# Turning k, q and x on VectorE in 32x32 squares instead of on TensorE

## The chip, the cores and the metric

The kernel runs on one core of one Trainium2 chip. The metric is the device time of one execution in microseconds (us). The clock that TensorE was granted differs a little from execution to execution (0.991 to 1.000 of full speed over the runs of the kernel before), and with it the time, by about 0.5%.

Names: PE is TensorE, ACT ScalarE, DVE VectorE, POOL GpSimd, and SP the engine whose queue issues nearly all DMA transfers. A "chunk" is 128 consecutive time steps of one batch entry; there are 24, counted from 0. The kernel works in steady blocks, one a chunk, from chunk 6 on; what comes before is the start.

## The reference

An mLSTM cell with a stabilised exponential gate, and behind it a feed-forward layer with a squared ReLU.

```python
B, H, S, D = 4, 8, 768, 40
for t in range(S):
    m_new = maximum(f_gate[t] + m, i_gate[t])
    f_stab, i_stab = exp(f_gate[t] + m - m_new), exp(i_gate[t] - m_new)
    C = f_stab * C + i_stab * outer(v[t], k[t])        # per batch entry and head
    n = f_stab * n + i_stab * k[t]
    y[t] = sigmoid(o_gate[t]) * (C @ q[t]) / maximum(abs(n @ q[t]), 1)
x = y.transpose(0, 2, 1, 3).reshape(B * S, H * D)      # 3072 x 320
h = maximum(x @ w_in, 0)                               # w_in 320 x 2048
out = (h * h) @ w_out                                  # w_out 2048 x 320
```

## The kernel before

The recurrence is computed chunk by chunk as attention with decay weights: scores of k and q, a product with the weights, and a state C carried from chunk to chunk. For the scores k and q are needed with the head dimension on the partitions, for the feed-forward layer x with its features there. TensorE makes all three by transposing against an identity matrix.

```python
def load(s):                      # k, q, v of one chunk, each [128 time steps, 8 heads, 40]
    b, c = divmod(s, NB)
    for dst, src in load_parts(s):
        nc.sync.dma_start(dst, src[b, :, c * P : (c + 1) * P, :].rearrange("h p d -> p h d"))

def transposes(s, o=(False, False)):
    d = st[s]
    for i, n in enumerate(("kT", "qT")):
        tp = bank(o[i])
        for j in range(PR):       # PR = 4 pairs of heads
            nc.tensor.transpose(tp[:, j, :], d["kq"][:, i, 2 * j : 2 * j + 2, :]..., ident[:])
        d[n] = work.tile([P, PR, P], F32, name=n)
        (nc.scalar.copy if ... else nc.vector.tensor_copy)(d[n][:], tp)

def turn_rows(s):
    ...
    for a in range(3):
        nc.tensor.transpose(tp[:, a, :], d["x"][:, a * P : (a + 1) * P], ident[:])
    nc.scalar.copy(st["xT", g][:, :, j * P : (j + 1) * P], tp[:])
```

The input weights arrive as raw words in 26 pieces, through a ring of buffers. ACT makes `mag` and `low` of a raw piece, DVE and POOL join them to a rounded fp32 piece, and then the next piece is fetched into the ring:

```python
def fetch(self):                  # next raw piece, on the SP queue
    ... nc.sync.dma_start(to, src)
def words(self):                  # ACT: abs and copy of the raw words -> mag, low
    ...
def join(self):                   # DVE x3, POOL x1 -> rounded piece; then
    ... self.fetch()

def attend_on(s):                 # second quarter of every steady block
    do(attend, s)
    do(normalise, s)
    do(load, s + 4)
    ...
for n, (which, g, i) in enumerate(parts):     # 4 quarters a block
    s, at = 6 + n // 4, n % 4
    ...
    if at == 1: attend_on(s)
    if at == 3:
        do(turn_rows, s)
        do(transposes, s + 1)
    ...                           # a quarter of the feed-forward products
    if n < 4:                     # chunk 6: the last pieces of the weights
        while rounding.done < NEXT[8 + n]:
            rounding.step()
```

So fetches of weights go on into chunk 6's block, on the same SP queue as all loads of chunks. The queue's timelines below show its issues in program order.

## Time and profile before

| | before |
|---|---|
| time, median of 3 | 568.83 us (568.2 to 569.38) |
| span of the profiled execution, granted clock | 565.8 us, 0.999 |
| PE busy | 554.9 us, 98% |
| one odd and one even block together | 44.1 us |
| scores of chunk 8 start at | 144.04 us |

PE is the bound: a product stands behind every other one and nothing waits, from 68 us on.

In the SP queue's timeline (start, duration of the issue, line, transfer) at the end of the start, the last piece of raw weights is issued like this:

```profile
104.77 0.57 SPq L268 DMA_DIRECT2D kq<-in_q_dram  x1
105.44 1.95 SPq L268 DMA_DIRECT2D va<-in_v_dram  x1
114.33 0.34 SPq L174 DMA_DIRECT2D raw<-in_moe_w_out_dram  x1
116.11 0.37 SPq L286 DMA_DIRECT2D A_bc<-a_rows  x1
```

The queue has nothing to do from 107.4 to 114.3 us: it is waiting for a ring buffer to come free (6.9 us behind DVE's last use of one, in the list of the queue's waits).

### The profile page before, as it was taken

The numbers are of one execution on the slowest core, as the hardware profiler recorded it, in microseconds if no ns is written. First come the engines' busy times: TensorE is split into PE (matmuls) and PEld (weight loads), VectorE is DVE, ScalarE is ACT, GpSimd is POOL, SyncE is SP. The second block draws the span as 40 slices with busy tenths as digits, with TensorE's granted clock in tenths as the row PEclk, the third lists the DMA queues.
The fourth block names the chain that finished last, engine by engine and source line by source line (L and its number), as shares of the span: only waits on it lengthen the run. The fifth ranks groups of instructions, "written<-read, shape, count | busy, mean of one in ns | idle before, by whom it ended". The sixth has DMA issues, their size and how long they took to land.

```text
span 565.8 us, 9740 instructions
## 1 busy us (share of the span) xinstructions
PE 554.9 (98%) x3878; PEld 497.8 (88%) x3879; DVE 312.0 (55%) x602; ACT 193.1 (34%) x483; POOL 98.1 (17%) x113
## 2 busy tenths in 40 slices
PE   9988899999999999999999999999999999999997
PEld 5876788887889989989989989989988998989997
DVE  8689978685554454455464364265356355434441
ACT  3767677353162033242131423223315105011000
POOL 3356543142112100111131120101211210000000
PEclk9999999999999999999999999999999999999999
DMA  9997989824313351233231433331411000000000
GB/s 193 222 215 166 171 191 202 169 60 85 57 39 48 79 91 25 64 81 48 61 66 39 89 48 62 73 58 38 76 34 38 1 23 2 1 24 0 25 24 23
DMA packets 130909, 42.60 MB, mean 75 GB/s; under 512 B 101072, under 2 KB 127696, under 8 KB 130864
## 3 DMA queue, kind: packets, MB, share of 16 engines
q1 hardware_dynamic: 130768, 41.79, 36.1%
q8 instruction: 30, 0.49, 0.4%
q10 hardware_dynamic: 96, 0.20, 0.1%
q14 instruction: 15, 0.12, 0.1%
HBM read 37.95 MB, written 4.03 MB: 74 GB/s over the span
## 4 chain that ended last, share of the span: by engine, by line
PE 92%; DVE 4%; ACT 1%; issue 1%; DMA 1%; POOL 0%; POOLq 0%; SPq 0%; DVEq 0%
PE h_ps L555 30%; PE h_ps L461 28%; PE h_ps L472 8%; PE hp L400 7%; PE tp L363 4%; PE tp L350 3%; PE h_ps L501 3%; PE dC L393 3%; PE hi L386 3%; PE tp L445 1%; PE idle L621 1%; PE A_ps L302 1%; ACT W_sb L326 1%; DVE mag L198 1%; PE A_ps L298 1%
## 5 line engine op out<-in xcount | busy, mean ns | idle before, releaser
L461 PE MATMUL h_ps<-xT,w_in 128*128 128x256 f32 x768 | 176.7, 383 | 2.3 <-POOL w_in L203 1.8
L461 PEld LDWEIGHTS h_ps<-xT,w_in 128*128 128x128 f32 x768 | 142.2, 190 | 25.1 <-issue 3.0
L487 ACT ACTIVATE r_sb<-h_ps 128x512 f32<-128x512 f32 x96 | 49.9, 601 | 173.8 <-PE h_ps L472 170.6
L494 DVE TENSOR_TENSOR g<-r_sb 128x512 f32<-128x512 f32 x96 | 62.4, 708 | 69.5 <-ACT r_sb L487 69.5
L555 PE MATMUL h_ps<-w_out,g 128*128 128x160 f32 x528 | 76.9, 302 | 0.0
L555 PEld LDWEIGHTS h_ps<-w_out,g 128*128 128x128 f32 x528 | 72.5, 190 | 1.3 <-ACT r_sb L487 0.3
L326 ACT ACTIVATE W_sb<-A_bc,b_T 128x128 f32<-128x128 f32 x176 | 53.8, 394 | 5.9 <-POOL A_bc L311 5.9
L555 PE MATMUL h_ps<-T,S 128*128 128x160 f32 x352 | 51.4, 299 | 0.0
L472 PE MATMUL h_ps<-xT,w_in 64*128 64x256 f32 x384 | 49.0, 391 | 0.0
L555 PEld LDWEIGHTS h_ps<-T,S 128*128 128x128 f32 x352 | 49.0, 190 | 0.0
L472 PEld LDWEIGHTS h_ps<-xT,w_in 64*128 64x128 f32 x384 | 34.8, 186 | 12.3 <-issue 9.3
L337 POOL TENSOR_TENSOR vw<-va,W_sb 128x328 f32<-128x328 f32 x20 | 16.6, 828 | 165.3 <-ACT W_sb L326 138.5
L400 PE MATMUL hp<-va,P_sb 128*128 128x41 f32 x368 | 44.1, 280 | 0.0
L400 PEld LDWEIGHTS hp<-va,P_sb 128*128 128x128 f32 x368 | 42.9, 192 | 0.0
L569 DVE TENSOR_TENSOR y_sb<-y_sb,h_ps 128x160 f32<-128x160 f32 x33 | 10.6, 320 | 55.1 <-PE h_ps L555 55.1
L419 POOL TENSOR_TENSOR C_sb<-C_sb,Cd 128x328 f32<-128x328 f32 x16 | 14.5, 904 | 140.1 <-DVE C_sb L411 139.9
L375 DVE TENSOR_TENSOR P_sb<-tp,W_sb 128x512 f32<-128x512 f32 x46 | 29.5, 683 | 13.0 <-PE tp L363 12.5
L569 DVE TENSOR_TENSOR y_sb<-h_ps,y_sb 128x160 f32<-128x160 f32 x22 | 7.1, 324 | 49.6 <-PE h_ps L555 30.9
L578 ACT COPY y_sb<-h_ps 128x160 f32<-128x160 f32 x11 | 3.2, 292 | 70.6 <-PE h_ps L555 70.6
L363 PEld LDWEIGHTS tp<-qT,kT 40*128 40x128 f32 x384 | 24.2, 187 | 3.3 <-issue 1.6
L363 PE MATMUL tp<-qT,kT 40*128 40x128 f32 x384 | 26.9, 279 | 0.0
L446 ACT COPY xT<-tp 128x384 f32<-128x384 f32 x24 | 11.4, 477 | 43.2 <-PE tp L445 43.2
(96 smaller groups left out, 682.5 us busy)
## 6 DMA issues: line engine op xcount, KB each, us to landing
A_bc<-a_rows SPq DMA_DIRECT2D x22, 512.0 KB, 4.4
raw<-in_moe_w_out_dram SPq DMA_DIRECT2D x16, 320.0 KB, 3.7
raw<-in_moe_w_in_dram SPq DMA_DIRECT2D x8, 512.0 KB, 5.2
kq<-in_k_dram SPq DMA_DIRECT2D x24, 160.0 KB, 4.4
kq<-in_q_dram SPq DMA_DIRECT2D x24, 160.0 KB, 4.9
va<-in_v_dram SPq DMA_DIRECT2D x24, 160.0 KB, 4.5
og<-in_o_gate_dram SPq DMA_DIRECT2D x24, 160.0 KB, 4.2
out_dram<-y_sb SPq DMA_DIRECT2D x24, 160.0 KB, 1.8
```

The costliest lines, as they stand in the source:

```text
L326: nc.scalar.activation(d["W"][:, i * n + h, :], A[i][:, h, :], AF.Exp, bias=b_T[:, b, c, i * n + h : i * n + h + 1],)
L350: nc.tensor.transpose(tp[:, j, :], d["kq"][:, i, 2 * j : 2 * j + 2, :].rearrange("p h d -> p (h d)"), ident[:],)
L363: nc.tensor.matmul(sc[i][:, j, :], lhsT=d["kT"][rows, j, :], rhs=d["qT"][rows, j, :], start=True, stop=True,)
L375: nc.vector.tensor_tensor(t, d["sc"][i], d["W"][:].rearrange("p (j two) t -> p j two t", two=2)[:, :, i, :], op=ALU.mult,)
L386: nc.tensor.matmul(hi[:, 2 * j : 2 * j + 2, :].rearrange("p h d -> p (h d)"), lhsT=d["qT"][:, j, :], rhs=C[:, j].rearrange("p h d -> p (h ...
L400: nc.tensor.matmul(hp[:, h, :], lhsT=d["P"][h % 2][:, h // 2, :], rhs=d["va"][:, h, :], start=True, stop=True,)
L461: nc.tensor.matmul(hs[i][:, n, :], lhsT=w_in[:, a, fb * P : (fb + 1) * P], rhs=xT[:, a, :], start=(n == 0 and a == 0), stop=False,)
L472: nc.tensor.matmul(hs[i][:, n, :], lhsT=w_in2[rows, 2 * pp + n, :], rhs=xT[rows, 2, :], start=False, stop=(n == 1),)
L487: nc.scalar.activation(rs[-1][:], h[:], AF.Relu)
L494: nc.vector.tensor_tensor(g4[:, :, i, :], r[:], r[:], op=ALU.mult)
L555: nc.tensor.matmul(to, lhsT=lhsT[:, p], rhs=rhs[:, p, :], start=(start and p == 0), stop=(p == NPAIR - 1), skip_group_check=True,)
L569: add = lambda to, a, b: nc.vector.tensor_tensor(to, a, b, op=ALU.add)
```

## The change

The intent is to take the transposes off PE. VectorE's transpose turns each 32x32 square in itself (the prediction names the page), so the loads put each square where it belongs, and one VectorE instruction then turns every square of a tile, those of k and x in place. For k and q, from chunk 7 on, a copy from DRAM to DRAM first sorts the rows by pairs of heads (`pair_up`), four loads for each of the two fetch the squares. For x, from chunk 6 on, the finished rows are stored to DRAM and fetched back as squares by four loads. Core of the diff:

```diff
+    def pair_up(s):
+        b, c = divmod(s, NB)
+        for n, src in enumerate((k, q)):
+            nc.sync.dma_start(
+                kq_d[s, n].rearrange("two j t d -> two j (t d)"),
+                src[b, :, c * P : (c + 1) * P, :].rearrange("(j two) t d -> two j (t d)", two=2),
+            )
+    def squares_in(s, n, dst):
+        for i in range(2):
+            for e in range(0, D, SQ):
+                ... nc.sync.dma_start(dst[...], kq_d[s, n, i, :, :, e : e + w].rearrange("j (m r) a -> r (j m) a", r=SQ))
+    def turn_kq(s):
+        nc.vector.transpose(kT, kT);  nc.vector.transpose(qT, q_squares(s))      # shortened
+    def store_rows(s):
+        nc.sync.dma_start(x_d[s]..., st[s]["x"]...)
+        for r in range(P // SQ):
+            nc.sync.dma_start(t[r * SQ : (r + 1) * SQ]..., x_d[s, :, :, r * SQ : (r + 1) * SQ]...)
+    def turn_squares(s):
+        nc.vector.transpose(t, t)
     def attend_on(s):
         do(attend, s)
         do(normalise, s)
+        do(store_rows, s)
+        do(load_kT, s + 2)
         do(load, s + 4)
+        do(pair_up, s + 5)
 ...  # the start, chunks 3 to 5
             load_A(s + 2)
+            for r in {3: (7, 8), 5: (9,), 7: (10,)}.get(u, ()):
+                pair_up(r)
             for r in {1: (4,), 3: (5, 6), 5: (7,), 7: ()}[u]:
                 load(r)
 ...  # the steady blocks
         if at == 3:
-            do(turn_rows, s)
-            do(transposes, s + 1)
 ...
         if at == 2:
             do(weigh_on, s + 1)
+            do(turn_kq, s + 1)
+        if at == 3:
+            do(turn_squares, s)
```

More of the change, by code (lines that the diff above doesn't have):

```diff
@@ L90 @@
     A_d = nc.dram_tensor("a_rows", (BH, S), F32, kind="Internal").ap()
+    kq_d = nc.dram_tensor("kq_rows", (NT, 2, 2, PR, P, D), F32, kind="Internal").ap()
+    x_d = nc.dram_tensor("x_rows", (NT, 3, P, P), F32, kind="Internal").ap()
     NKQ = 4
@@ L95 @@
     va_b = [consts.tile([P, H, D1], F32, name=f"va{i}") for i in range(NKQ)]
+    NKT = 3
+    kT_b = [consts.tile([P, PR, P], F32, name=f"kT{i}") for i in range(NKT)]
     ident = consts.tile([P, P], F32)
@@ L263, in load_parts, with q_squares, load_kT @@
         return (kq[:, 0, :, :D], k), (kq[:, 1, :, :D], q), (va[:, :, :D], v)
+    SQ = 32
+    KQ_SQ, X_SQ = 7, 6
+    def pair_up(s):
[8 more added lines that the diff above has]
+            for e in range(0, D, SQ):
+                w = min(SQ, D - e)
+                nc.sync.dma_start(
+                    dst[DP * i + e : DP * i + e + SQ].rearrange("p (b a) -> p b a", a=SQ)[:, :, :w],
+                    kq_d[s, n, i, :, :, e : e + w].rearrange("j (m r) a -> r (j m) a", r=SQ),
+                )
+    def q_squares(s):
+        return kq_b[s % NKQ][:, 1].rearrange("p h d -> p (h d)")
     def load(s):
         b, c = divmod(s, NB)
-        for dst, src in load_parts(s):
+        (dk, sk), nat_q, vv = load_parts(s)
+        for dst, src in ((dk, sk), nat_q, vv) if s < KQ_SQ else ((dk, sk), vv):
             nc.sync.dma_start(dst, src[b, :, c * P : (c + 1) * P, :].rearrange("h p d -> p h d"))
+        if s >= KQ_SQ:
+            if s < KQ_SQ + NKQ:
+                nc.gpsimd.memset(q_squares(s), 0.0)
+            squares_in(s, 1, q_squares(s))
+    def load_kT(s):
+        t = st[s]["kT"] = kT_b[s % NKT]
+        squares_in(s, 0, t[:].rearrange("p j t -> p (j t)"))
+    def turn_kq(s):
+        d = st[s]
+        nc.vector.transpose(d["kT"][:].rearrange("p j t -> p (j t)"), d["kT"][:].rearrange("p j t -> p (j t)"))
+        d["qT"] = work.tile([P, PR, P], F32, name="qT")
+        nc.vector.transpose(d["qT"][:].rearrange("p j t -> p (j t)"), q_squares(s))
     def load_o(s):
@@ L352, in transposes @@
                 )
-            d[n] = work.tile([P, PR, P], F32, name=n)
+            d[n] = work.tile([P, PR, P], F32, name=n) if i else kT_b[s % NKT]
             (nc.scalar.copy if i == 0 or s in (0, *range(2, 7)) else nc.vector.tensor_copy)(d[n][:], tp)
@@ L436, in normalise, with xT_half @@
         nc.vector.tensor_copy(x[:, DM:], x[:, DM - KR : DM])
+    def xT_half(s):
+        g, j = divmod(s, GT)
+        if j == 0:
+            st["xT", g] = xts.tile([P, GT, 3, P], F32, name="xT")
+        return st["xT", g][:, j]
+    def store_rows(s):
+        t = st[s]["xT"] = xT_half(s).rearrange("p c t -> p (c t)")
+        nc.sync.dma_start(x_d[s].rearrange("c t d -> t c d"), st[s]["x"][:].rearrange("p (c d) -> p c d", c=3))
+        for r in range(P // SQ):
+            nc.sync.dma_start(
+                t[r * SQ : (r + 1) * SQ].rearrange("p (b a) -> p b a", a=SQ),
+                x_d[s, :, :, r * SQ : (r + 1) * SQ].rearrange("c (n p) a -> p (c n) a", p=SQ),
+            )
+    def turn_squares(s):
+        t = st[s]["xT"]
+        nc.vector.transpose(t, t)
+        del st[s]
     def turn_rows(s):
         d = st[s]
-        g, j = divmod(s, GT)
-        if j == 0:
-            st["xT", g] = xts.tile([P, 3, WG], F32, name="xT")
+        t = xT_half(s)
         tp = ps_at.tile([P, 3, P], F32, name="tp", tag="at")
@@ L445, in turn_rows @@
             nc.tensor.transpose(tp[:, a, :], d["x"][:, a * P : (a + 1) * P], ident[:])
-        nc.scalar.copy(st["xT", g][:, :, j * P : (j + 1) * P], tp[:])
+        nc.scalar.copy(t, tp[:])
         del st[s]
@@ L461, in ffn1_main @@
                     nc.tensor.matmul(
-                        hs[i][:, n, :], lhsT=w_in[:, a, fb * P : (fb + 1) * P], rhs=xT[:, a, :],
+                        hs[i][:, n, :], lhsT=w_in[:, a, fb * P : (fb + 1) * P], rhs=xT[:, :, a, :],
                         start=(n == 0 and a == 0), stop=False,
@@ L472, in ffn1_rest @@
                 nc.tensor.matmul(
-                    hs[i][:, n, :], lhsT=w_in2[rows, 2 * pp + n, :], rhs=xT[rows, 2, :],
+                    hs[i][:, n, :], lhsT=w_in2[rows, 2 * pp + n, :], rhs=xT[rows, :, 2, :],
                     start=False, stop=(n == 1),
@@ L609, in attend_on @@
         do(normalise, s)
+        do(store_rows, s)
+        do(load_kT, s + 2)
         do(load, s + 4)
+        do(pair_up, s + 5)
         if 8 <= s < 20:
             load_o(s + 4)
-    zeros = consts.tile([P, W], BF16)
+    zeros = consts.tile([P, 16], BF16)
     nc.vector.memset(zeros[:], 0.0)
@@ L620, in idle @@
         for _ in range(n):
-            nc.tensor.matmul(t[:], lhsT=zeros[:, :P], rhs=zeros[:], start=True, stop=True)
+            nc.tensor.matmul(
+                t[:], lhsT=zeros[:, :1].to_broadcast([P, P]), rhs=zeros[:, :1].to_broadcast([P, W]), start=True, stop=True,
+            )
     def fetch(n):
@@ L746 @@
     load_A(8)
+    load_kT(7)
     banks.close()
```

## The prediction

> **What bounds the kernel now.** I read the page first, then the chain of waits, then TensorE's timeline of one stretch of the main loop, then the waits and the DMA issues. Busy time and the chain agree on TensorE:
>
> ```profile
> PE 554.9 (98%) x3878; PEld 497.8 (88%) x3879; DVE 312.0 (55%) x602; ACT 193.1 (34%) x483; POOL 98.1 (17%) x113
> ...
> PEclk9999999999999999999999999999999999999999
> DMA  9997989824313351233231433331411000000000
> ...
> PE 92%; DVE 4%; ACT 1%; issue 1%; DMA 1%; POOL 0%; POOLq 0%; SPq 0%; DVEq 0%
> ```
>
> PE is busy 98% of the span at full clock and makes up 92% of the chain that ended last. In the chain, listed in order of time, the other engines' 8% lies before 68 us, where the weights are rounded; after that it is PE and nothing else. So any PE time that is removed after 68 us shortens the kernel one for one, unless something new makes PE wait. The DMA row matters too: eight slices (0 to 113 us) are nearly full, the rest is at a third.
>
> A busy PE row says nothing of the cost of one transpose, because matmuls overlap (274 ns each, by the list of groups). The timeline of TensorE, one line for each run of equal work, gives the spacing:
>
> ```profile
> 227.53 2.34 PE L555 MATMUL h_ps<-T,g 128*128 128x160 f32 x16
> 229.71 0.49 PE L445 MATMUL tp<-ident,x_sb 128*128 128x128 f32 x3
> 230.03 1.04 PE L350 MATMUL tp<-ident,kq 128*128 128x128 f32 x8
> 230.91 2.34 PE L555 MATMUL h_ps<-w_out,S 128*128 128x160 f32 x16
> 233.18 1.16 PE L363 MATMUL tp<-qT,kT 40*128 40x128 f32 x16
> 234.27 3.72 PE L461 MATMUL h_ps<-xT,w_in 128*128 128x256 f32 x16
> ```
>
> First column is the start. The three transposes of x (L445) start at 229.71, those of k and q (L350) at 230.03, the next matmuls at 230.91: 0.32 and 0.88 us. The chain has the same pieces as 0.33 and 0.87. So one chunk's transposes cost PE 1.20 us, 109 ns each.
>
> **What the Trainium skill says.** (1) "TensorE: Matmul & The Clock Gate", part 4, "PE-mode transpose": about 275 ns in a kernel's context, and the result lands in PSUM, so a copy must follow. The trace agrees: 274 ns, and copies of 586 ns (ACT, kT), 689 ns (DVE, qT) and 477 ns (ACT, xT). The 275 is a latency; the price here is the 109 ns of spacing. (2) "VectorE: DVE Perf Modes", "The three transpose paths": VectorE turns 32x32 blocks only, from SBUF to SBUF. Hence the loads must put the squares in their places. No transpose on VectorE is in this trace. (3) The same page's section on the TRN2 errata fits fp32 tensor_tensor as (N+151)/0.96 ns, 691 ns for N = 512; the trace's 128x512 square takes 708 and the P product 683. I use that form as an estimate for the VectorE transpose: 0.69 us for 512 columns, 0.56 us for x's 384. (4) "DMA: Bandwidth & Descriptors", "Why a DMA increments its semaphore by 16 and not by 1": a transfer is spread over the largest k up to 16 that divides both sides' slowest dimension. The new DRAM-to-DRAM copy of k or q has 2 on one side and 8 on the other, so k = 2: two of the 16 engines carry all of it. No run shows this yet.
>
> **The change part by part.** The built programs, compared, confirm the counts: transposes of k and q go from 192 to 56, those of x from 72 to 18.
>
> Removed from PE: 17 chunks (7 to 23) x 0.87 = 14.8 us, and 18 chunks (6 to 23) x 0.33 = 5.9 us; together 20.7 us, all after 110 us, where the chain is PE alone. From 568.8 that leaves 548.1. Also gone are ACT's copies (17 x 0.59 + 18 x 0.48 = 19 us, of an engine at 34%) and DVE's 17 copies of qT, all off the path.
>
> Added to DVE, per chunk: 2 x 0.69 + 0.56 - 0.69 = 1.25 us, 22 us in all. DVE is busy 8 to 9 us of the 20-us blocks and 12 to 14 us of the 23-us blocks of the main loop; it has room. The transposes of k and q stand after the third quarter of a block and serve the next block's scores, their loads being issued a block earlier: no wait.
>
> Added to DMA, per chunk. The packet records of the trace, by size, have medians of 14 ns (160 bytes), 27 (512), 55 (1280) and 159 (4096). Before, a chunk moves 4096 packets of 160 bytes (k, q, v, o), 1024 of 512 (A) and 128 of 1280 (out). By the means (18, 29 and 59 ns) that is 74 + 30 + 8 = 112 us of engine time, over 16 engines 7 us of the 21.6-us mean block: 0.32, and the windows show 0.31 for the block at 233 us. The change takes q's 1024 packets away and adds 1024 x 2 squares of 128 bytes and 1024 x 2 of 32 bytes for k and q, 1536 of 128 for x, 384 of 512 for the store of x, and two copies of 8 rows of 20480 bytes. Estimating 13 ns for 128 bytes and 11 for 32: -18 + 27 + 23 + 20 + 11 + 13 = +76 us, some 190 in all, 12 us an engine in a 20.4-us block. But the two engines with the row copies have 8 x 0.8 = 6.4 us of rows (20480 bytes at the 26 bytes/ns of the 4096-byte packets, an estimate) on top of about 11: 17.4 of 20.4 us. That fits, barely.
>
> The new round trip of x is what PE could wait for. For an odd chunk the next block's first matmuls need it. VectorE finished such an x here:
>
> ```profile
> 222.67 0.49 DVE L435 TENSOR_TENSOR x_sb<-x_sb,dm 128x320 f32<-128x320 f32 x1
> 223.20 0.19 DVE L436 COPY x_sb<-x_sb 128x64 f32<-128x64 f32 x1
> ...
> 233.28 0.32 DVE L569 TENSOR_TENSOR y_sb<-y_sb,h_ps 128x160 f32<-128x160 f32 x1 [1.49 <-PE h_ps L555]
> ```
>
> x is done at 223.4. In the changed order its transpose stands right after the last line shown, which ends at 233.6 and will end 1.2 us earlier without the transposes: 232.4. So 9.0 us are left for the store and the four loads. The page's last part shows what such transfers take:
>
> ```profile
> kq<-in_k_dram SPq DMA_DIRECT2D x24, 160.0 KB, 4.4
> ...
> out_dram<-y_sb SPq DMA_DIRECT2D x24, 160.0 KB, 1.8
> ```
>
> Last column: us from issue to landing. The store is like the second: 2.2 us with its 384 runs. The loads each have 384 packets, not the 1024 of the first line; the last is issued some 1.6 us after the store lands (issues are 0.37 to 0.57 us on the SP queue) and lands about 2.5 us later. Sum 6.3 us, 2.7 us of room. Then VectorE's 0.56 us begins 0.42 us after the end of PE's last product and PE's scores (1.1 us) run meanwhile; a hand-over of 0.1 to 0.2 us is left, in 9 odd blocks: 1.4 us lost. Even chunks have a whole block more.
>
> The start: four pairs of row copies are put in at about 60 to 95 us, where DMA is full, and on two engines they add 4 x 6.4 = 26 us. What it delays are raw weights and A. The wait list has one DMA wait of 0.4 us for raw weights and one of 1.5 for A, so most of the slack is there, but SP sits idle only from 107 to 114 us to catch up. I allow 2 us.
>
> Sum: 568.8 - 20.7 + 1.4 + 2 = 551.5 us.
>
> **The rivals.** First, the two loaded engines become the bound. If a 20480-byte row from DRAM to DRAM takes 1.3 us and not 0.8, they have 8 x 1.3 + 11 = 21.4 us per 20.4-us block, everything that spans 16 engines lands at their pace, and the gain shrinks by 1 us a block: 565 us or, with x late too, slower than before. For: 16-KB instruction packets average 1.16 us here. Against: those share engines with the full queues of the start. I give it 10%. Second, x comes late by other means (store and loads together over 9 us, because they queue behind the previous block's row copies): each microsecond costs 9 us, so 555 to 562. Against: 23 us lie between an even block's x and the next odd one's, longer than the 17 us of transfers. 12%. Third, the start is DMA bound in earnest and loses 5 to 10 us: 555 to 559. 12%. Fourth, VectorE's fp32 transpose is twice as slow as estimated (1.3 us and 1.1): hand-over 0.7 us, 9 x 0.6 = 5 us, 557. Fifth, nothing waits and PE's own small waits for transposed rows go as well: 547 to 548.
>
> **Range and chances.** Without trouble 548 to 552, with one of the middle rivals 555 to 560. Predicted 551.5, 80% range 547.5 to 560. Over 2% faster means below 557.5: 0.78. Within 2%: 0.17. Slower: 0.05, the saturated engines.
>
> **What would show it.** PE's busy time should fall by about 20 us with its share still 97 to 98%. In TensorE's timeline the pieces L445 and L350 should vanish with no gap in their place. VectorE's three transposes should read 0.69, 0.69 and 0.56 us. The DMA share of the main loop should rise from 0.3 to about 0.6. The store of x should land in about 2.2 us and the loads within 6.5 us of it. I am wrong if PE's main matmuls on xT wait for VectorE by more than 0.3 us a block, if the row copies land later than about 8 us, or if the first 130 us grow by more than 4 us.

## The result, and the profile after

| | before | after |
|---|---|---|
| time, median of 4 runs | 568.53 us (568.2 to 569.38) | 582.72 us (582.08 to 583.88) |
| ratio, 95% interval | | 1.025 (1.0228 to 1.0271): slower |
| span of the profiled execution, granted clock | 565.8 us, 0.999 | 582.1 us, 0.965 |

A ratio here is the mean time of one kernel's runs over that of the other's of the same rounds, so it is not quite the ratio of the medians quoted beside it.

The page after (busy row of PE; granted clock and DMA share in 40 slices of 14.6 us; the chain that ended last):

```profile
PE 547.4 (94%) x3688; PEld 487.2 (84%) x3689; DVE 329.2 (57%) x637; ACT 176.9 (30%) x448; POOL 99.6 (17%) x117
...
PEclk9988998897579999999999999999999999999999
DMA  9996486776043626644644654554573021100000
...
PE 80%; DVE 6%; DMA 5%; ACT 4%; SPq 2%; issue 1%; POOL 1%; DVEq 0%; ACTq 0%; POOLq 0%
```

From the fourteenth slice on (189 us) all is as planned: full clock, DMA at about half. Before that the clock dips to 5 and 7, the DMA row has holes (4 in the fifth slice, where it was 9 before, and 0 in the eleventh), and the chain has 5% of DMA where it had 1%. So split the span. The starts of the scores (one run of 16 matmuls on kT and qT a chunk), read from PE's timelines of the two kernels, in us:

| scores of chunk | before | after | difference |
|---|---|---|---|
| 3 | 48.09 | 51.25 | +3.2 |
| 4 | 67.97 | 68.56 | +0.6 |
| 5 | 83.37 | 86.39 | +3.0 |
| 6 | 97.87 | 106.66 | +8.8 |
| 7 | 120.86 | 130.63 | +9.8 |
| 8 | 144.04 | 176.62 | +32.6 |
| 23 | 479.39 | 493.91 | +14.5 |
| end of span | 565.8 | 582.1 | +16.3 |

Chunks 8 to 23 gained 18.1 us. The transposes removed in between are 15 of k and q at 0.87 us and 15 of x at 0.33 us, 18.0 us by the sizes of the prediction: all of it arrived. Everything was lost, and more, before chunk 8's scores: 32.6 us, and 35.0 if one counts the 2.4 us that two chunks' removed transposes should have saved there. The 1.8 us that are added behind chunk 23's scores are small: 0.90 is the wait for x shown below, and about 1 lies behind PE's last product (3.2 us from its end to the end of the span before, 4.2 after).

**The steady part.** PE's timeline after, the same stretch of a block as in the prediction (products, then scores, then the next block's products on xT):

```profile
216.95 2.34 PE L619 MATMUL h_ps<-w_out,S 128*128 128x160 f32 x16
219.22 1.16 PE L409 MATMUL tp<-qT,kT 40*128 40x128 f32 x16
220.31 3.72 PE L525 MATMUL h_ps<-xT,w_in 128*128 128x256 f32 x16
```

The transposes are gone and nothing waits in their place: from the scores at 219.22 to those two blocks on is 41.71 us (260.93), before it was 44.11 (233.18 to 277.29), 2.40 less. VectorE's transposes, in the list of groups (the number behind the comma is the mean in ns of one, then idle time ahead of them):

```profile
L312 DVE STREAM_TRANSPOSE kT<-kT 128x512 f32<-128x512 f32 x17 | 12.0, 704 | 0.5 <-DMA kT<-kq_rows 0.5
L314 DVE STREAM_TRANSPOSE qT<-kq 128x512 f32<-128x512 f32 x17 | 11.4, 670 | 0.0
L501 DVE STREAM_TRANSPOSE xT<-xT 128x384 f32<-128x384 f32 x18 | 10.3, 573 | 1.6 <-DMA xT<-x_rows 1.6
```

Only at the very end, where no scores stand between x and the products on it, does PE wait for one of them:

```profile
513.96 7.17 PE L525 MATMUL h_ps<-xT,w_in 128*128 128x256 f32 x32 [0.90 <-DVE xT L501]
```

**The start.** The list of waits (who waits for what: us in total, times, longest) gives the reason in one line, ahead of the same line of the kernel before:

```profile
ACT mag L188 <- DMA raw<-in_moe_w_out_dram: 37.9, 6, 16.1
```

```profile
ACT mag L183 <- DMA raw<-in_moe_w_out_dram: 0.4, 1, 0.4
```

The raw weights are late, six times. Where that begins is seen in the SP queue's timeline after, at the first four row copies (chunks 7 and 8):

```profile
60.95 1.44 SPq L278 DMA_DIRECT2D kq_rows<-in_k_dram  x1
62.44 0.64 SPq L278 DMA_DIRECT2D kq_rows<-in_q_dram  x1
63.12 0.60 SPq L278 DMA_DIRECT2D kq_rows<-in_k_dram  x1
63.76 0.60 SPq L278 DMA_DIRECT2D kq_rows<-in_q_dram  x1
64.46 0.38 SPq L300 DMA_DIRECT2D kq<-in_k_dram  x1
64.88 8.90 SPq L300 DMA_DIRECT2D kq<-in_q_dram  x1
73.88 3.49 SPq L300 DMA_DIRECT2D va<-in_v_dram  x1
```

An ordinary load of q takes 8.90 us to issue, with no wait on record: the queue stands, and what is behind it is not issued. In the kernel before, the same loads of the same chunk were issued like this:

```profile
60.29 1.40 SPq L268 DMA_DIRECT2D kq<-in_k_dram  x1
61.73 1.33 SPq L268 DMA_DIRECT2D kq<-in_q_dram  x1
```

The packet records of the trace show what was under way: the 32 rows of 20480 bytes of these four copies, 761 ns each in the median, ran two at a time from 64.2 to 77.2 us, as two of 16 engines would. Apart from them, 0.16 MB moved from 65 to 69 us and 8 bytes from 69 to 73 us; in the same stretches before it was 0.58 and 0.68 MB. The activity of 60 to 75 us shows what the 16 DMA engines did meanwhile (fields: window, length, busy time and count of PE, PEld, DVE, ACT, POOL, then clock, DMA share, GB/s), first before, then after:

```profile
60.00:75.00 15.00, 12.61 (x84) 10.14 (x83) 13.83 (x25) 8.56 (x23) 6.50 (x8) 1.00 1.11 185
```

```profile
60.00:75.00 15.00, 13.14 (x89) 10.67 (x88) 14.27 (x25) 8.23 (x23) 6.75 (x7) 1.00 0.44 121
```

In the very stretch in which the transfers were to be packed, the share of busy DMA falls from 1.11 to 0.44. (The recorded times of transfers overlap, hence over 1.) The same recurs behind the later row copies: 8.41 us for four issues at 87.29 and 6.33 us for one at 107.25.

The last piece of raw weights then comes into a queue that is busy with the steady part's new transfers, instead of idle as before:

```profile
127.35 0.38 SPq L492 DMA_DIRECT2D x_rows<-x_sb  x1
131.31 1.86 SPq L494 DMA_DIRECT2D xT<-x_rows  x4
133.22 2.06 SPq L288 DMA_DIRECT2D kT<-kq_rows  x4
...
138.83 0.62 SPq L278 DMA_DIRECT2D kq_rows<-in_k_dram  x1
139.49 0.61 SPq L278 DMA_DIRECT2D kq_rows<-in_q_dram  x1
140.21 0.36 SPq L179 DMA_DIRECT2D raw<-in_moe_w_out_dram  x1
```

It is issued at 140.21 us and not at 114.33. The chain that ended last runs through these new transfers, the store's landing and the issues, from 127.35 to 140.21 us, and then has the piece of weights as 9.11 us, right behind two row copies. ACT waits for it with the ReLU of the feed-forward layer behind it in order (ACT's timeline), VectorE's squares and its product P wait for that, and PE for P (PE's timeline):

```profile
149.40 0.48 ACT L188 ACTIVATE mag<-raw 128x320 f32<-128x320 f32 x1 [16.06 <-DMA raw<-in_moe_w_out_dram]
```

```profile
155.61 1.97 PE L439 MATMUL dC<-vw,kq 128*128 128x82 f32 x8 [18.56 <-DVE P_sb L421]
157.37 3.55 PE L446 MATMUL hp<-va,P_sb 128*128 128x41 f32 x16
160.72 15.97 PE L565 MATMUL h_ps<-w_out,g 128*128 128x320 f32 x48
```

18.56 us of PE idle, and the work behind it at half pace: 1.97 and 3.55 us for runs that take 1.06 and 1.92 in the steady part. The granted clock is 0.50 from 139.1 to 166.3 us, so it stays there for 10.7 us after PE has work again. So between chunk 7's scores and chunk 8's lie 45.99 us, where before lay 23.18. The 32.6 us are thus 9.8 up to chunk 7's scores and 22.8 in the block behind them.

A small part of the +32.6 may not be the change's. The +3.2 us at chunk 3 stand before the first row copy; there the granted clock was 0.83 from 40 to 60 us. The kernel of experiment e3, which is the kernel before up to 60 us, shows nearly the same (chunk 3's scores at 50.96). It is a matter of the single execution, and I don't explain it. Little of it lasts: at chunk 4 it is +0.6, and in e5 and e6 below, without two-engine copies, +5.0 and +2.6 at chunk 3 have become +1.3 and 0.0 at chunk 4. About 1 us of the 32.6 can come from there.

### The profile page after: what moved, and what is told of

It is laid out like the page before. It is cut to its first block, busy times and chain, and to the rows that moved or that the text cites. A ratio compares the mean times of both kernels' runs of the same rounds, so it can differ in the third digit from the quotient of the medians.

```text
span 582.1 us, 9738 instructions
## 1 busy us (share of the span) xinstructions
PE 547.4 (94%) x3688; PEld 487.2 (84%) x3689; DVE 329.2 (57%) x637; ACT 176.9 (30%) x448; POOL 99.6 (17%) x117
## 4 chain that ended last, share of the span: by engine, by line
PE 80%; DVE 6%; DMA 5%; ACT 4%; SPq 2%; issue 1%; POOL 1%; DVEq 0%; ACTq 0%; POOLq 0%
PE h_ps L619 29%; PE h_ps L525 23%; PE hp L446 7%; PE h_ps L536 6%; DMA raw<-in_moe_w_out_dram 4%; PE tp L409 3%; PE dC L439 3%; PE h_ps L565 3%; PE hi L432 2%; SPq L288 1%; DVE g L558 1%; DVE mag L203 1%; PE idle L688 1%; ACT W_sb L372 1%; ACT mag L188 1%
## 5 line engine op out<-in xcount | busy, mean ns | idle before, releaser
L525 PE MATMUL h_ps<-xT,w_in 128*128 128x256 f32 x768 | 179.4, 390 | 5.8 <-ACT xT L510 2.7
L525 PEld LDWEIGHTS h_ps<-xT,w_in 128*128 128x128 f32 x768 | 145.7, 194 | 30.4 <-ACT xT L510 3.1
L558 DVE TENSOR_TENSOR g<-r_sb 128x512 f32<-128x512 f32 x96 | 64.1, 727 | 72.0 <-ACT r_sb L551 72.0
L446 PE MATMUL hp<-va,P_sb 128*128 128x41 f32 x368 | 47.3, 292 | 0.0
L446 PEld LDWEIGHTS hp<-va,P_sb 128*128 128x128 f32 x368 | 46.3, 204 | 0.0
L383 POOL TENSOR_TENSOR vw<-va,W_sb 128x328 f32<-128x328 f32 x20 | 16.3, 813 | 160.0 <-ACT W_sb L372 134.2
L439 PE MATMUL dC<-vw,kq 128*128 128x82 f32 x160 | 22.2, 284 | 19.6 <-DVE P_sb L421 19.6
L439 PEld LDWEIGHTS dC<-vw,kq 128*128 128x128 f32 x160 | 20.6, 199 | 20.2 <-issue 19.9
```

The source lines that it names most:

```text
L439: nc.tensor.matmul(dC[:, j].rearrange("p h d -> p (h d)"), lhsT=d["kq"][:, 0, 2 * j : 2 * j + 2, :].rearrange("p h d -> p (h d)"), rhs=d[" ...
L446: nc.tensor.matmul(hp[:, h, :], lhsT=d["P"][h % 2][:, h // 2, :], rhs=d["va"][:, h, :], start=True, stop=True,)
L525: nc.tensor.matmul(hs[i][:, n, :], lhsT=w_in[:, a, fb * P : (fb + 1) * P], rhs=xT[:, :, a, :], start=(n == 0 and a == 0), stop=False,)
L558: nc.vector.tensor_tensor(g4[:, :, i, :], r[:], r[:], op=ALU.mult)
```

## The experiments

Two theories, each with a different cure. Theory A, the shape: a row copy has a slowest dimension of 2, runs on two of the 16 engines, and stops the whole queue behind it; spread it over 16 engines and the loss is gone. Theory B, the order: the last raw weights stand behind chunk 6's new transfers of x, k and q in the queue; put them first and the loss is gone. The expectations also weigh a theory C, too many small packets in a full start; e4, which keeps every small packet, refutes it. Later experiments take up which half of the change gains what, and what the half clock costs.

**e1_spread: the row copies over 16 engines.** Four transfers a chunk instead of two, each of 64 runs of 1280 bytes in 16 groups; the bytes are the same.

```diff
-            nc.sync.dma_start(kq_d[s, n]... "two j t d -> two j (t d)", src...)
+            for i in range(2):
+                nc.sync.dma_start(
+                    kq_d[s, n, i].rearrange("j t d -> j (t d)").rearrange("j (p e) -> p j e", p=16),
+                    src...[i].rearrange("j (p e) -> p j e", p=16))
```

> The changed kernel with each row copy cut so that both sides have 16 as the slowest dimension (four transfers of 64 pieces of 1280 bytes a chunk in place of two of 8 rows of 20480 bytes); nothing else. Theory A (two loaded DMA engines hold up everything behind them): the issue of q for the chunk after the first copies falls from 8.9 us to under 3, ACT's waits for raw weights from 37.9 us to under 10, the time to 550-558 us. Theory B (the order on the SP queue: the last raw weights stand behind the first round trip of x): the 16-us wait for raw weights and the 18.6-us wait of TensorE stay at 8 us or more, time 565-575 us. Theory C (too many small packets in a full start): waits hardly change, 578 us or more.

Measured: 563.01 us (562.41 to 564.76), ratio 0.9913 (0.9887 to 0.9939). That is 19.7 us less than the changed kernel, and between the theories: A alone would have it at 550 to 558, and the waits for raw weights under 10 us. The queue no longer stands, as its timeline behind the copies shows:

```profile
66.03 0.53 SPq L302 DMA_DIRECT2D kq<-in_k_dram  x1
66.61 0.58 SPq L302 DMA_DIRECT2D kq<-in_q_dram  x1
```

```profile
ACT mag L188 <- DMA raw<-in_moe_w_out_dram: 14.2, 4, 12.6
```

But one wait for raw weights of 12.6 us stays, with a PE wait of 9.5 us behind it, at the same place as before: chunk 7. Chunk 8's scores start at 155.50. The shape is a large part and not all.

**e2_raw_first: chunk 6's moves after the last raw piece.** The row copies stay on two engines.

```diff
     def attend_on(s):
         do(attend, s)
         do(normalise, s)
+        if s > 6:
+            moves(s)
+    def moves(s):
         do(store_rows, s)
         do(load_kT, s + 2)
         do(load, s + 4)
         do(pair_up, s + 5)
 ...
             while rounding.done < NEXT[8 + n]:
                 rounding.step()
+            if n == 1:
+                moves(6)
```

> The changed kernel with the new transfers of chunk 6 (store and loads of x, squares, row copies) put after the last fetch of raw weights in the same quarter block, row copies still on two engines. Theory B: the 16-us wait goes, with it TensorE's 18.6-us gap and most of the halved clock behind it, time 552-558 us. Theory A: the waits for raw weights before 130 us (6.2, 4.0, 6.3 us) stay, since the early copies stay; only the last wait shrinks; time 558-567 us. Theory C: over 575 us.

Measured: 565.54 us (563.1 to 569.72, in two pairs: 563.1 and 563.27, 567.81 and 569.72), ratio 0.996 (0.9903 to 1.0017), 17.2 us less than the changed kernel. Waits for raw weights 20.2 us in 4, the longest now 6.5; the 18.56-us wait at chunk 7 has shrunk to 1.41. The early standing of the queue remains (chunk 8's scores at 160.59). Again a large part, not all.

**e4_spread_raw: both.**

> Both edits, spread copies and raw weights first. Theories A and B together: no wait over 3 us left for raw weights, no stretch at half clock after 60 us, time 549-553 us, which is the predicted gain. Theory C: still over 565 us.

Measured: 549.95 us (548.4 to 552.53, 5 runs), ratio 0.9674 (0.965 to 0.9699): faster than the kernel before. Against the changed kernel that is -32.8 us, where the two alone make -19.7 and -17.2; the two sum to 36.9, so they overlap by about 4 us (e2's runs alone differ by 6.6). No third cause of any size is left: at chunk 8's scores it lacks 3.5 us of what two chunks' removed transposes should have saved. The page, and the waits:

```profile
PE 538.0 (98%) x3689; PEld 480.3 (87%) x3689; DVE 329.9 (60%) x637; ACT 176.7 (32%) x448; POOL 99.9 (18%) x117
...
PEclk9998989999999999999999999999999999999999
```

```profile
ACT mag L188 <- DMA raw<-in_moe_w_out_dram: 5.9, 3, 3.1
```

Two expectations were narrowly missed: one wait of 3.1 us is left, and the granted clock was 0.50 from 69.5 to 72.9 us. Chunk 8's scores start at 145.09, 1.1 us after those of the kernel before, and the rest of the span takes 405.6 us, as in the changed kernel (582.1 - 176.62 = 405.5). So the cure lies wholly in the start, and the row copies on two engines cost the steady part nothing.

**e3_dead_copies and e11_dead_spread: the kernel before, with copies that nobody reads.** The early row copies alone, eight of them, put into the kernel before: on two engines in e3, over 16 in e11. This tells the shape from the bytes, without the rest of the change.

```diff
             load_A(s + 2)
+            for r in {3: (7, 8), 5: (9,), 7: (10,)}.get(u, ()):
+                pair_up(r)          # e3: as in the change; e11: as in e1
```

> The kernel before with nothing new but the eight early row copies (chunks 7 to 10, two engines), which nobody reads. Theory A: they alone delay the start, waits of ACT for raw weights and the gate rise from 0.4 us to 5-20 us in all, time 574-585 us. Theories B and C: without the round trip of x and the small packets it stays within 2 us of the kernel before, 568-571 us.

Measured: 579.53 us (578.47 to 580.35) beside 567.98 of the kernel before in the same rounds, ratio 1.0198 (1.0172 to 1.0224): 11.5 us for eight transfers of no use. The same load of q stands, and the raw weights are late:

```profile
64.43 8.88 SPq L278 DMA_DIRECT2D kq<-in_q_dram  x1
```

```profile
ACT mag L193 <- DMA raw<-in_moe_w_out_dram: 17.5, 5, 6.7
```

All of it is lost before chunk 7's scores (131.71, 10.9 us later than before; from there to the end 445.0 us, before 444.9), where the changed kernel has 9.8. So the early copies account for the first part of the loss. In the second part, chunk 7's block, 13.1 of the 22.8 us remain when the copies are spread (e1, 36.23 us where before lay 23.18) and 3.7 when the raw weights go first (e2, 26.92 us, though its chunk 7's scores come 3.0 us later): there the order is the larger part.

> The kernel before with the same early copies that nobody reads, now over 16 engines: the same bytes, sixteen times shorter pieces, twice the transfers. If it is the two engines and not the bytes or the number of transfers, it stays within 3 us of the kernel before, 568-571 us, where the two-engine copies cost 11.5 us. If it is the bytes: 576-581 us.

Measured: 569.08 us (568.19 to 569.92) beside 568.89, ratio 1.0004 (0.9984 to 1.0023), waits for raw weights 0.6 us, and the load of q is issued in 0.58 us (at 66.40). The same bytes at the same places in the queue cost nothing that shows when they are cut for 16 engines. This settles theory A for the first part of the loss: it is the shape and not the load. The cut also makes the pieces sixteen times shorter; which of the two, more engines or shorter pieces, keeps the queue moving was not tested apart.

**e5_x_only and e6_kq_only: half of the change each,** both with the cures of e4. In e5 k and q are transposed on PE as before, in e6 x is.

```diff
 # e5: no row copies, no squares of k and q
-    KQ_SQ, X_SQ = 7, 6
+    KQ_SQ, X_SQ = NT, 6
         if at == 3:
+            do(transposes, s + 1)
-            do(turn_kq, s + 1)
 # e6: no store and no squares of x
-        do(store_rows, s)
         if at == 3:
+            do(turn_rows, s)
-            do(turn_squares, s)
```

> The repaired kernel (spread copies, raw weights first) with only x on VectorE; k and q stay on TensorE in every chunk. By the spacing of the trace of the kernel before, x's 54 transposes are worth 18 x 0.33 = 5.9 us; less some 1.5 us for the hand-over in 9 odd blocks: 563-565 us beside 568 before. A rival (each transpose is worth its 274 ns, since its latency counts): 54 x 0.27 = 15 us, 553 us.

> The repaired kernel with only k and q on VectorE; x stays on TensorE. By the spacing 17 x 0.87 = 14.8 us, less up to 1 us at the start: 553-555 us. Together with the run before, the two gains should add up to that of the repaired kernel (18 us) within 1.5 us.

Measured: x alone 563.33 us (ratio 0.9907, 0.9881 to 0.9933), 4.7 us under the kernel before; k and q alone 553.02 us (0.9734, 0.9707 to 0.9761), 15.0 us under. Together 19.7, and e4 gained 18.0 in all, so the two are near independent (1.7 us apart, where 1.5 were expected at most). The three transposes of x are worth about a third of the eight of k and q, as their 0.33 and 0.87 us say; the rival that each is worth its 274 ns (553 us for x alone) is refuted.

**e7_late: two-engine copies, but none early.** The row copies are as in the change; k and q go by squares from chunk 12 on only, and chunk 6's moves come after the raw weights.

```diff
-    KQ_SQ, X_SQ = 7, 6
+    KQ_SQ, X_SQ = 12, 6
-        do(pair_up, s + 5)
+        if s + 5 >= KQ_SQ:
+            do(pair_up, s + 5)
```

> The changed kernel with raw weights first, row copies on two engines as they were, but k and q on VectorE only from the thirteenth chunk, so that no row copy or square falls in the start. If the copies hurt in the full start alone, their two-engine form costs nothing in the main loop: 12 x 0.87 + 5.9 = 16.3 us less 2 us, 553-555 us, 11 us under the same kernel with early copies (565.5). If two-engine copies also slow the main loop, over 558 us.

Measured: 553.16 us (552.51 to 553.68), ratio 0.9734 (0.9713 to 0.9755). The shape that costs some 20 us in the full queues of the start is harmless in the steady part: this kernel is faster than the one before with every copy on two engines.

**e8_warm, e9_warm7 and e12_warm_hi: what the half clock costs.** These add matmuls of zeros to the changed kernel, so that PE stays busy while it would wait.

```diff
     def attend_on(s):
+        if s == 6:                    # e8; e9: s == 7
+            idle(80)
 # e12, before chunk 7's first products into the bank hi:
+            if s == 7:
+                for _ in range(110):
+                    nc.tensor.matmul(hi[:]..., lhsT=zeros..., rhs=zeros..., start=True, stop=True)
```

> The changed kernel as it was, with 80 matmuls on zeros put ahead of chunk 6's state product, where TensorE waited 18.6 us. If that wait is what halves the clock, the 27 us at half clock shrink to under 7, the matmuls behind it return to 1.06, 1.92 and 13 us from 1.97, 3.55 and 16 us, and the time falls by about 5 us to 576-579 us. If the clock falls for another reason, it stays 581-584 us.

> The 80 matmuls on zeros moved to where the 18.6-us wait really was, ahead of chunk 7's products (the run before had them ahead of chunk 6's, where they only pushed everything back). Expected as then: if the wait halves the clock, the stretch of 27 us at half clock goes, the matmuls behind the wait take 1.06, 1.92 and 13 us, and the time is 576-579 us beside 582.7 of the changed kernel. If the clock falls for another reason: 581-584 us.

> The third try at the clock: 110 matmuls on zeros (328 columns, some 16 us) written into the bank of chunk 7's state product just before it overwrites that bank. This bank is free when TensorE comes to it, where the run before took a bank that came free only with the late data, waited 12.6 us for it and then did its 20 us of zeros on top. If the idle stretch halves the clock: no half clock behind it, products of 1.0, 1.9 and 13 us in place of 1.97, 3.55 and 16, time 576-579 us. If not: 581-584 us.

Measured: e8 591.51 us, ratio 1.0406 (1.0379 to 1.0434). A miss of my own making: the long wait is in chunk 7's block, and the filler in chunk 6's only pushed 17.67 us of work back. e9, 594.84 us, ratio 1.0453 (1.0432 to 1.0475), has it in the right block, but the filler itself needs a buffer that only the late ReLU frees:

```profile
150.92 19.88 PE L690 MATMUL idle<-zeros 128*128 128x512 bf16 x80 [12.64 <-ACT r_sb L551]
```

So it waited, and then ran on top. e12 writes into a bank that is free already, and does what was meant (PE's timeline):

```profile
140.75 15.80 PE L433 MATMUL hi<-zeros 128*128 128x328 bf16 x110
156.39 1.01 PE L438 MATMUL hi<-C_sb,qT 128*128 128x82 f32 x8
158.57 1.09 PE L445 MATMUL dC<-vw,kq 128*128 128x82 f32 x8 [1.16 <-DVE P_sb L421]
159.50 2.03 PE L452 MATMUL hp<-va,P_sb 128*128 128x41 f32 x16
161.33 14.77 PE L571 MATMUL h_ps<-w_out,g 128*128 128x320 f32 x48
```

With PE kept busy the granted clock is 1.00 from 139 to 161 us, where it was 0.50, and the same runs take 1.09, 2.03 and 14.77 us instead of 1.97, 3.55 and 15.97 (the third has 3.4 us at half clock in it, from 161.2 us). That the wait halves the clock is shown, and it agrees with the Trainium skill ("TensorE: Matmul & The Clock Gate", Part 1, "What's actually happening": back to half after one idle window of about 3.4 us). The sum of the three is 3.6 us less: so much, at least, the half clock costs behind the wait. (From chunk 7's scores to chunk 8's it is 40.67 us instead of 45.99, but this is no second measure: the stretch began 4.7 us later, and the awaited P came only 3.0 us later.) But the total, 582.44 us (580.3 to 584.29), ratio 1.0224 (1.0188 to 1.026), is only 0.3 us under the changed kernel's, where 576 to 579 were expected: a miss. In the profiled execution chunk 7's scores began 4.7 us later (135.35 instead of 130.63), why is not shown. What the half clock costs of the total stays open; behind this wait 3.6 us are measured, and the 18.56 us of waiting ahead of it are the larger part either way.

**e10_best: e4 with x on VectorE from chunk 8 on only,** to keep its store and loads out of the last of the start.

```diff
-    KQ_SQ, X_SQ = 7, 6
+    KQ_SQ, X_SQ = 7, 8
```

> The repaired kernel with x on VectorE only from the ninth chunk, so that the first two round trips of x, which fall among the last raw weights, go too. The run with k and q alone lost nothing at the start (third block at 142.3 us), the repaired one reaches it at 145.1 and takes 405.6 us from there: 142.3 + 405.6 = 547.9 us of span, 546.5-548.5 us timed, 2 to 3 us under the repaired kernel. If the 3 us at the start are not the first round trips of x, 549-551 us.

Measured: 549.3 us (548.63 to 550.88), ratio 0.9657 (0.9639 to 0.9676). The lowest median of all kernels here, faster than the kernel before and the changed one, but 0.7 us under e4 is within the scatter, and the expectation was not met. That the first two moves of x still cost something once the raw weights come first is not shown. The traces put e4's lost time elsewhere: at chunk 5's scores, before any move of x, e4 and e10 are already 2.45 and 2.17 us later than the kernel before, each with a stretch of 3.4 us at half clock from 69.5 and 69.7 us on; e6, whose program is e4's up to there, is not late at all (83.33 us, before 83.37) and has the clock at 1.00. So it is a matter of the single execution.

## Why the prediction was wrong

It said 551.5 us, faster; it was 582.72, slower by 2.5% than the kernel before. By its own steps:

- **What bounds the kernel: right.** PE time removed in the steady part came off the span one for one.
- **Removed from PE, 20.7 us: right.** From chunk 8's scores to chunk 23's, 18.1 us were gained, against 18.0 by these sizes; in e5 and e6 the halves gave 4.7 and 15.0 us, against 5.9 less hand-over and 14.8.
- **Added to DVE: right.** 704, 670 and 573 ns stand against 0.69, 0.69 and 0.56 us, and no block waits for them.
- **Added to DMA in the steady part: right in what it decides.** The share is 0.52 and 0.54 in the windows from 243 to 263 and 263 to 286 us (0.6 estimated). The 20480-byte rows took 761 ns in the median (0.8 estimated), and e7 shows that two engines can bear them there.
- **The hand-over of x, 1.4 us in 9 odd blocks: too high by a little.** None in the steady blocks, 0.90 us once at the end.
- **Two slips in its figures, without consequence.** The mean block before is 22.4 us (335.35 us from chunk 8's scores to chunk 23's, over 15), not 21.6, so the two engines have some 21 us for their 17.4; and the median of the 4096-byte packets is 162 ns, not 159.
- **The start, "I allow 2 us": this is the step that failed.** It measured 35.0 us, of which about 1 may be the chance of the clock. The size of the added load was right (8 copies of 8 rows at 761 ns over two engines are 24 us, 26 in the prediction). Wrong was the reading of what it delays. "Most of the slack is there" took the short waits of the kernel before for room, one transfer at a time. Short waits say that transfers came just in time; how much later they might have come, they don't say. And the lateness is not confined to two engines: the SP queue is in order and during one standing issue of 8.90 us next to nothing else moved on all 16 (8 bytes from 69 to 73 us), so the start lost DMA time rather than gaining a load. The queue's idle stretch between chunk 6's loads and the last raw piece (107 to 114 us before), which the prediction counted on for catching up, was filled by the steady part's new transfers, and the last raw piece went behind them: 26 us late at its issue (8.8 of them because the block came late, by chunk 6's scores), 18.56 us of PE wait. The early copies alone cost 11.5 us (e3); with both cures all but 3.5 of the 35 us are gone (e4).

Of the rivals, the first had the mechanism, two loaded engines at whose pace everything lands, and put it in the steady part, where it did not happen. The third had the place, the start, and 5 to 10 us for it. Neither joined the two. The check that it gave itself, "if the first 130 us grow by more than 4 us", came out at 9.8 us by chunk 7's scores, and the larger loss followed.

With the start repaired (e4) the kernel takes 549.95 us: what the prediction had worked out for the steady part holds.

## What to carry to other kernels

Before adding transfers to a queue, list what stands behind them in program order and on how many DMA engines each runs: transfers on two of 16 engines in a full queue hold up everything behind them, and the same bytes with a slowest dimension of 16 may cost nothing (11.5 us against 0.2 here for eight copies). A small wait in the profile is not slack; slack is the time from a transfer's landing to its first use. And when a change gains in the steady part, compare the start and the steady part separately, by a mark that both kernels have.

## What the Trainium skill lacked or had wrong

- "DMA: Bandwidth & Descriptors", "Why a DMA increments its semaphore by 16 and not by 1": the rule for how many engines a transfer uses fits what was seen (rows two at a time), and the page advises all 16. It does not say what a transfer on few engines does to the full-width ones behind it in the same queue: an issue of 1.33 us became 8.90, the DMA share of the stretch fell from 1.11 to 0.44, and eight such copies cost 11.5 us, spread over 16 engines 0.2.
- The same page, "Issuing engines are not separate DMA queues": the sequencer's time for an issue is "usually small relative to the DMA itself". In this start single issues took 8.90 and 6.33 us, longer than the 4.4 to 4.9 us that such loads took from issue to landing before.
- "VectorE: DVE Perf Modes", "The three transpose paths": it has 311 ns for 128x128 bf16 only, and no page has a measured time in fp32. In fp32, as 32x32 squares, 128x512 took 670 to 704 ns and 128x384 573 ns.
- "TensorE: Matmul & The Clock Gate", Part 4: the 275 ns there (for bf16; 274 here in fp32) are the time of one transpose and not its price among others. Taking away eleven a block shortened two blocks by 2.40 us, 109 ns each.
- The same page, Part 1: it has the clock fall after an idle window. In the changed kernel the granted clock was 0.52 and 0.51 from 40 to 43 and 43 to 47 us, although PE had been busy for 2.31 of the 3.4 us before; in the kernel before it had been busy for 2.32 us of them, and the clock stayed at 1.00. The page does not tell how much work in a window counts as idle, and no run here does.
